# Linear attention and a two-layer feed-forward on one core: weight blocks kept for a third chunk, half of x without a trip through memory, one combination kept in PSUM, and a new hand-written order

## Chip, cores and metric

One Trainium2 chip, one core of it. The metric is the device time of one execution in microseconds (us). Kernel before: 828.3 us, the median of 3 runs (825.68 to 830.06). The profile and the trace are of one execution of 824.08 us, whose span is 822.3 us.

Names of the engines: PE is TensorE (matmuls), PEld its weight loads, DVE VectorE, ACT ScalarE, POOL GpSimd, SP the engine that issues every DMA of this kernel.

## What is computed

```python
def _attn_ref(q, k, v):                      # batch 8, heads 8, seq 576, head_dim 64
    q_s = np.exp(q - np.max(q, axis=-1, keepdims=True))
    q_s = q_s / (np.sum(q_s, axis=-1, keepdims=True) + 1e-09)
    k_s = np.exp(k - np.max(k, axis=2, keepdims=True))
    k_s = k_s / (np.sum(k_s, axis=2, keepdims=True) + 1e-09)
    kv = np.einsum('bhsd,bhse->bhde', k_s, v)
    return np.einsum('bhsd,bhde->bhse', q_s, kv)

def _moe_ref(x, w_in, w_out):                # x 4608 x 512, w_in 512 x 2048, w_out 2048 x 512
    h = x @ w_in
    g = np.where(h >= 1, h, np.where(h <= -1, 0.0, (h + 1) ** 2 / 4))
    return g @ w_out
```

The output of the attention, 4608 tokens by 512, is the x of the feed-forward. All of it is fp32.

## The kernel before

**The work.** The 4608 tokens go in 9 chunks of 512. An fp32 operand is split into a high and a low part (fp32r), and each product is made of three matmuls (high by high, high by low, low by high), so the feed-forward is 3168 matmuls of 128x512 on PE. w_in is cut into 16 blocks f of 512 KB (both parts), w_out likewise.

- *Chunk 0* makes the parts of the weights: `weights` (L561) loads raw w_in and w_out (`st<-in_w`), scales and splits them (ACT L614 the high part, POOL L618 the low part), and stores most blocks to memory. Blocks 1, 3, 5, 7, 9, 11 of w_in stay in rooms of SBUF that x will need later (HELD, L69) until chunk 1 has used them; the other ten are stored and loaded again for chunk 1, and all sixteen for chunk 2, `w<-b` (`fetch`, L671).
- *Chunks 0 to 2* are computed plainly: `first_layer` (matmuls L1499, bank h), the middle (relu ACT L1651, square ACT L1655 or POOL L1657, min and max DVE L1661), `second_layer` (split ACT L1684 and DVE L1687, matmuls L1696, banks o).
- *Chunks 3 to 8* go in pairs (3,4), (5,6), (7,8) by Strassen's scheme in Winograd's form, seven products in place of eight. `two_first_layers` (L1531) computes for each of 8 units p the products P1, P2, P5, P6, P3, P7, P4 into three PSUM banks: A is `h{p%2}`, C is `h{1-p%2}`, B is `hb`. In the notes of the trace they are hA, hC and hb. What is C for one unit is A for the next. DVE adds the results (L1582); `combinations` (L1737) does the same for the second layer (split L1786, L1789, matmuls L1801 into oA and oX, sums L1836).
- For this the sums of weight blocks are needed (`sums`, L757): sw, ss, then the split w_s (ACT L740, DVE or POOL L744), stored as s (L788) and loaded as `w<-s`. They are made in chunks 1 and 2 from the blocks that are in SBUF then.

**x.** `attention_two` (L1215) makes k's maxima (L1250), turns them (`mt`, L1256), stores them and loads them spread over the partitions (`mk<-mt` L1260, `m<-mk` L1268), subtracts (L1277), takes exp (L1283), sums kv on PE (L1293) and scales it (z L1304, L1306, kvt L881 and L879); `x_two` (L883) multiplies (L903). For chunks 3 to 8 x goes from PSUM to a tile xo (ACT L473 or DVE L475), from there to memory (`xk<-xo`, L936), and back into the five slots of xc, of which there is one buffer (`xc<-xk`, L1161); from xc come seven differences and copies (L1176), split into the rooms x0 to x13 (ACT L1188, DVE or POOL L1193).

**Buffers.** Five rooms of 512 KB serve w (pool ws); x rooms x0 to x13 hold x of chunks 0 to 2 (x0 to x3, x4 to x7, x10 to x13) and HELD blocks.

**The order.** The program first lists its operations with a home engine each, and then `Plan.settle` (L413) emits them in the order of a hand-written list, SEQUENCE, that holds the numbers of the operations of all engines in one row. A second list, SECOND, names those that go to their other engine. Nothing reorders at run time: an engine takes its operations in this order, and waits at each until what it needs is there.

```python
        for n in SECOND:
            self.ops[n].engine = self.ops[n].ways[1][0]
        done = set()
        for n in SEQUENCE:
            assert done.issuperset(d.n for d in self.ops[n].deps)
            done.add(n)
        return [self.ops[n] for n in SEQUENCE]
```

## Time and profile before

| | |
|---|---|
| median of 3 runs | 828.3 us (825.68 to 830.06) |
| profiled execution, its span | 824.08 us, 822.3 us |
| granted clock of PE, mean | 0.996 |
| PE busy | 792.0 us (96%) |
| PEld busy | 631.5 us (77%) |
| DVE busy | 605.8 us (74%) |
| ACT busy | 479.4 us (58%) |
| POOL busy | 439.7 us (53%) |
| DMA | 213.35 MB, 76.7% of 16 DMA engines' span in the main queue |

The table says which engines have much to do, not which one sets the end: a busy share is an average over chunk 0, the plain chunks and the pairs. Matmuls are pipelined and their ends are modelled, so "busy" of PE is not a measure of its pace. Which wait ends last is read from the timeline and the chain of waits.

### The profile page before, as it was taken

To read this page: it belongs to the slowest core of one execution; us is meant where nothing else is said; L and a number is where in the kernel's file an instruction comes from. 1 tells how busy PE (TensorE), PEld (TensorE's weight loads), DVE (VectorE), ACT (ScalarE), POOL (GpSimd) and SP (SyncE) were. 2 spreads that over 40 slices of the span, in tenths; PEclk is the share of its full clock that TensorE was granted. 3 is DMA by queue.
4 is the path that set the end of the run, shared out by engine and by line. 5 is a ranking of instruction groups with operands and counts; after the bars stand their busy time and mean duration, and the time that the engine had idled before them with its cause. 6 is when DMAs were issued, how large, how long until landed. Compare 5 with 4: busy or idle time off the path is not lost.

```text
span 822.3 us, 12384 instructions
## 1 busy us (share of the span) xinstructions
PE 792.0 (96%) x4136; PEld 631.5 (77%) x4136; DVE 605.8 (74%) x1024; ACT 479.4 (58%) x906; POOL 439.7 (53%) x358
## 2 busy tenths in 40 slices
PE   7999999999899999989999999999999999999997
PEld 6677777778586778767787778787877888888886
DVE  6787879777567767877877897778669764755684
ACT  6876865356545564567476755555657454455553
POOL 5545555354456656554666633474762644673633
PEclk9999999999999999999999999999999999999999
DMA  9788988888889897988898666686667675575546
GB/s 327 249 283 274 309 294 284 299 308 276 282 267 324 308 315 273 305 299 267 274 330 276 204 225 226 251 307 229 244 206 238 214 236 184 193 268 192 179 153 205
DMA packets 83232, 213.35 MB, mean 259 GB/s; under 512 B 9440, under 2 KB 17376, under 8 KB 83168
## 3 DMA queue, kind: packets, MB, share of 16 engines
q1 hardware_dynamic: 83168, 212.55, 76.7%
q8 instruction: 33, 0.54, 0.3%
q14 instruction: 31, 0.25, 0.1%
HBM read 165.31 MB, written 47.20 MB: 258 GB/s over the span
## 4 chain that ended last, share of the span: by engine, by line
PE 67%; DMA 16%; DVE 5%; ACT 4%; issue 3%; POOL 2%; SPq 2%; DVEq 0%; POOLq 0%; ACTq 0%
PE hA L1558 14%; PE oA L1801 14%; PE oX L1801 11%; PE h L1499 8%; PE hC L1558 8%; PE o L1696 6%; PE hb L1558 3%; DMA w<-s 3%; DMA st<-in_w 3%; PE x L903 2%; DMA q<-in_q 2%; DMA w_P<-v_P 1%; PE kv L1293 1%; DMA w<-b 1%; DMA m<-mk 1%
## 5 line engine op out<-in xcount | busy, mean ns | idle before, releaser
L1558 PE MATMUL hA<-x,w 128*128 128x512 f32 x576 | 144.6, 391 | 0.4 <-DMA w<-s 0.3
L1801 PE MATMUL oA<-g_P,w_P 128*128 128x512 f32 x576 | 141.1, 390 | 0.0
L1801 PEld LDWEIGHTS oA<-g_P,w_P 128*128 128x128 f32 x576 | 107.6, 188 | 24.1 <-ACT x L1188 0.8
L1558 PEld LDWEIGHTS hA<-x,w 128*128 128x128 f32 x576 | 107.6, 188 | 24.1 <-DMA w<-s 1.3
L1696 PE MATMUL o<-wh,g 128*128 128x512 f32 x384 | 119.9, 392 | 0.3 <-DVE g L1687 0.3
L1499 PE MATMUL h<-x,w 128*128 128x512 f32 x432 | 113.1, 395 | 2.0 <-ACT xo L473 1.2
L1789 POOL TENSOR_TENSOR g_P<-g,g_P 128x512 fp32r<-128x512 f32 x54 | 76.3, 1420 | 66.7 <-ACT g_P L1786 60.7
L1786 ACT CAST g_P<-g 128x512 fp32r<-128x512 f32 x120 | 72.9, 618 | 66.9 <-PE oA L1801 20.4
L1801 PE MATMUL oX<-g_P,w_P 128*128 128x512 f32 x432 | 106.7, 391 | 1.8 <-DMA w_P<-v_P 1.8
L1499 PEld LDWEIGHTS h<-x,w 128*128 128x128 f32 x432 | 80.4, 189 | 22.3 <-ACT xo L473 1.8
L1801 PEld LDWEIGHTS oX<-g_P,w_P 128*128 128x128 f32 x432 | 80.6, 188 | 20.1 <-ACT g_P L1786 2.5
L1696 PEld LDWEIGHTS o<-wh,g 128*128 128x128 f32 x384 | 72.5, 189 | 16.7 <-DVE g L1687 2.0
L1558 PE MATMUL hC<-x,w 128*128 128x512 f32 x288 | 74.3, 393 | 5.1 <-DMA w<-s 2.5
L1696 PE MATMUL o<-wl,g 128*128 128x512 f32 x192 | 76.4, 398 | 2.2 <-ACT g L1684 2.1
L1655 ACT ACTIVATE r<-r 128x512 f32<-128x512 f32 x109 | 68.4, 630 | 1.1
L1558 PEld LDWEIGHTS hC<-x,w 128*128 128x128 f32 x288 | 53.4, 188 | 19.5 <-DVE g L1661 3.0
L1657 POOL TENSOR_TENSOR r<-r 128x512 f32<-128x512 f32 x35 | 39.3, 1122 | 48.9 <-ACT r L1651 48.9
L1789 DVE TENSOR_TENSOR g_P<-g,g_P 128x512 fp32r<-128x512 f32 x66 | 52.8, 806 | 13.4 <-ACT g_P L1786 13.1
L1409 POOL TENSOR_TENSOR q<-q,qmb 128x512 f32<-128x512 f32 x32 | 37.4, 1181 | 40.3 <-DVE qmb L1391 35.6
L1409 POOL TENSOR_TENSOR q<-q,qzb 128x512 f32<-128x512 f32 x32 | 35.2, 1109 | 39.5 <-DVE qzb L1431 34.3
L1651 ACT ACTIVATE r<-c,half 128x512 f32<-128x512 f32 x48 | 34.2, 721 | 37.3 <-DVE c L1582 36.1
L1789 POOL TENSOR_TENSOR g_P<-c,g_P 128x512 fp32r<-128x512 f32 x27 | 38.0, 1410 | 28.3 <-ACT g_P L1786 28.2
(144 smaller groups left out, 1461.1 us busy)
## 6 DMA issues: line engine op xcount, KB each, us to landing
w_P<-v_P SPq DMA_DIRECT2D x84, 512.0 KB
w<-b SPq DMA_DIRECT2D x50, 512.0 KB
w<-s SPq DMA_DIRECT2D x48, 512.0 KB
st<-in_w SPq DMA_DIRECT2D x32, 512.0 KB
v<-in_v SPq DMA_DIRECT2D x32, 325.0 KB
q<-in_q SPq DMA_DIRECT2D x36, 256.0 KB
kt<-in_kt SPq DMA_DIRECT2D x32, 288.0 KB
...
```

The source lines that it names most:

```text
L903: nc.tensor.matmul(t[r][cols, :, p0:p1], kvt[rows, g % NKV, pr, :], q[pr]["tq"][rows, :, p0:p1], start=True, stop=True, tile_position=(r * ...
L1293: nc.tensor.matmul(kv[d, i, :], t[pr]["k"][:, j, d], t[pr]["v"][:, j, e * (D + 1) : (e + 1) * (D + 1)], start=(j == 0), stop=(j == KJ - 1) ...
L1409: nc.gpsimd.tensor_tensor(qf, qf, at, alu)
L1499: nc.tensor.matmul(t["h"], lhs, rhs, start=(turn == 0 and i == 0), stop=(turn == NPAIR - 1 and i == 2),)
L1558: nc.tensor.matmul(banks[b]["h"], lhs, rhs, start=(begins and not kk and not m), stop=(ends and kk == 1 and m == 2), skip_group_check=True,)
L1651: nc.scalar.activation(t["r"], t["h"], AF.Relu, bias=half[:, :1], scale=0.5)
L1655: nc.scalar.activation(t["r"], t["r"], AF.Square)
L1657: nc.gpsimd.tensor_tensor(t["r"], t["r"], t["r"], ALU.mult)
L1696: nc.tensor.matmul(outs[c, j], t["g"][:, k, s], rhs, start=(begins and i == 0), stop=(closes and i == 2),)
L1786: nc.scalar.copy(t["g"][:, 0, :], tile_of(i, b))
L1789: by(engine).tensor_tensor(t["g"][:, 1, :], tile_of(i, b), f32(t["g"][:, 0, :]), ALU.subtract)
L1801: nc.tensor.matmul(banks[side, d], wr[c, group, k, i // 2][:, i % 2, w, d * P : (d + 1) * P], t["g"][:, g, :], start=(begins and w == 1), ...
```

## The change

1. **KEPT.** Blocks 2, 4, 6, 8 of w_in are loaded in chunk 1 into x rooms 0 to 3 (which x of chunk 0 has left) and, with the held blocks 9 and 11, stay for chunk 2 (STAY). Six loads of 512 KB in chunk 2 are left out, and these blocks take none of the five rooms of w.
2. **Half of x straight.** For the first half (h = 0) of each chunk 3 to 8, ACT or DVE copies x from PSUM into its slot of xc (`x_straight`); 12 stores and 12 loads of 256 KB are left out. The one buffer of xc is taken from then on.
3. **12 stays in PSUM.** The sum P3 + U2 was written to a slot in SBUF, after which bank C was free. Now it is written in place in bank C, the middle for it reads PSUM and writes a slot, and bank C is free only after the min.
4. **More ways.** The low part of the weights (L618) and the row operations of q (L1409) may run on DVE: by the new SECOND 7 of 32 and 15 of 64 do. DVE has 1055 instructions where it had 1024, ACT 898 (901), POOL 328 (356), SP 574 (604). The matmuls are the same.
5. **A new order.** SEQUENCE and SECOND are new from end to end.

```diff
 HELD = {1: 10, 3: 11, 5: 12, 7: 13, 9: 8, 11: 9}
+KEPT = {2: 0, 4: 1, 6: 2, 8: 3}
+STAY = {9: 8, 11: 9, **KEPT}
...
 SEQUENCE = (
-    1, 0, 20, 86, 93, 44, 63, 11, 2, 19, 12, 43, 100, 3, 13, 62, 30, 4, 14, 31, 6, 21, 87, 88,
...
+    20, 1, 44, 0, 19, 86, 345, 93, 43, 63, 62, 11, 21, 30, 12, 100, 31, 54, 2, 3, 55, 32, 13,
...
-        def low():
+        def low(engine):
             hi, lo = parts()
-            nc.gpsimd.tensor_tensor(lo, whole(), f32(hi), ALU.subtract)
+            by(engine).tensor_tensor(lo, whole(), f32(hi), ALU.subtract)
...
-        g = op("POOL", 1.31, due, low, [e], port=True)
+        g = op("POOL", 1.31, due, low, [e], port=True, other=vector)
...
+    def fetch_kept(f, due):
+        r = ring(f"x{KEPT[f]}", 1)
...
+            wr[1, f] = wr[2, f] = flat.rearrange("p (q i t) -> p q i t", q=2, i=2)
+            nc.sync.dma_start(f32(wr[1, f]), blocks[f])
...
+        o = plan.read(0.45, due, emit, [made["stored", f], *r.wait()], 512)
...
             if c == 1 and f in HELD:
                 made[c, f] = made[f, 0]
+            elif c == 1 and f in KEPT:
+                made[c, f] = fetch_kept(f, due - 1.5 * STEP)
+            elif c == 2 and f in STAY:
+                made[c, f] = made[1, f]
             else:
...
+        def x_straight(r):
+            kk = two[r]
...
+            def emit(engine):
+                if c == base and not kk:
+                    xcs[base] = rp.tile([P, 5, T], F32, tag="xc", name=f"xc_{c}_0", bufs=1)
+                copy_by(engine, xcs[base][:, (3 * kk, kk + 1)[c - base], :], flat(r))
...
+            if not h:
+                rxc, begins = ring("xc", 1), c == base and not kk
+                waits = rxc.wait() if begins else [xdone[base, 0]]
+                ways = [("DVE", 0.69, False)]
+                xo = do("ACT", 0.59, due + 1, x_straight(r), xm, *waits, other=ways)
...
-        qs = do("POOL", 1.04, 1, q_rows("qm", ALU.subtract), qm, port=True)
+        qs = do("POOL", 1.04, 1, q_rows("qm", ALU.subtract), qm, port=True, other=vector)
...
-        c12, c22 = {}, {}
+        c22 = {}
...
-        o12 = dve(spilled(c12, "c12", s12), h["C"], lambda: side["U2"], due + 8.4, p3, u2, *r12.wait())
-        r12.take(o12)
-        rc.free(o12)
+        o12 = dve(h["C"], h["C"], lambda: side["U2"], due + 8.4, p3, u2)
...
-            for i, (x, b) in enumerate(((three, "12"), (four, "22"))):
-                d = middle(c + 1, f + i, due + 14 + 4 * i, *x[:2], kept=True)
-                unit[b] = x[0], d, x[2]
+            place = take_slot()
+            d = middle(c + 1, f, due + 14, *three, place=place)
+            ring(f"ps h{1 - p % 2}", 1).free(d)
+            unit["12"] = three[0], d, place
```

**What stands where, before and now.** Three places. The first is DVE's list of operations in chunk 1, about the step that scales kv of head group 4_0 (z, rz, kvt), for which PE waits with the next x. Before:

```order
L925 TENSOR_TENSOR x12_2472<-x_2_1_0_2453,x12_2472 128x512
L1424 TENSOR_REDUCE qs_4_0_2491<-q_4_0_2353 128x16
L1277 TENSOR_TENSOR k_3_3_2423<-k_3_3_2423,m2_3_1_2464 128x640
L1424 TENSOR_REDUCE qs_4_0_2491<-q_4_1_2368 128x16
L1304 TENSOR_SCALAR z_4_0_2536<-kv_4_0_2494 128x2
L1306 RECIPROCAL rz_4_0_2538<-z_4_0_2536 128x2
L881 TENSOR_SCALAR kvt_95<-kv_4_0_2494,rz_4_0_2538 128x64
L1661 SCALAR_TENSOR_TENSOR h_1_14_2409<-h_1_14_2409,r_1_14_2516 128x512
```

Now (in the changed file the lines are some 30 to 55 further down: L1353 is L1304, L1326 is L1277):

```order
L788 TENSOR_TENSOR sw_1_2490<-x0_1483 128x512
L1713 SCALAR_TENSOR_TENSOR h_1_14_2367<-h_1_14_2367,r_1_14_2426 128x512
L1353 TENSOR_SCALAR z_4_0_2521<-kv_4_0_2493 128x2
L1355 RECIPROCAL rz_4_0_2523<-z_4_0_2521 128x2
L905 TENSOR_SCALAR kvt_95<-kv_4_0_2493,rz_4_0_2523 128x64 x2
L1473 TENSOR_REDUCE qs_4_0_2531<-q_4_0_2378 128x16
L1739 TENSOR_TENSOR g2_1_14_2516<-h_1_14_2367,g2_1_14_2516 128x512
L1473 TENSOR_REDUCE qs_4_0_2531<-q_4_1_2411 128x16
L480 COPY qzo_4_0_2562<-qs_4_0_2531 32x32 x4
```

The subtraction of group 3_3 (`k_3_3<-k_3_3,m2_3_1`), which needs a load of m, stood ahead of z; now the two subtractions with m2_3_1 stand 15 and more rows behind it, and both halves of kvt are DVE's (one was ACT's).

The second place is SP's list at the start of the first pair. s7_0 and s7_1 are the stores of the last two weight sums; w_3_0_0 to w_3_0_3 are the weights of the pair's first unit (b0, s0_0, s0_1, b1), and xc_3_1 the second filling of xc. Before:

```order
L1240 DMA q_6_1_3654<-in_q 128x512
L1260 DMA mk6_0_176<-mt_6_0_3539 4x32
L788 DMA s7_1_144<-w_s_7_1_3634 128x1024
L675 DMA w_3_0_1_3668<-s0_0_129 128x1024
L1240 DMA v_6_0_3673<-in_v 128x650
L1268 DMA m2_6_0_3698<-mk6_0_176 128x256
L653 DMA v1_P2_153<-wh13_992 128x256
L675 DMA w_3_0_2_3712<-s0_1_130 128x1024
L675 DMA w_3_0_3_3714<-b1_114 128x512
```

Now:

```order
L811 DMA s7_0_143<-w_s_7_0_3490 128x1024
L811 DMA s7_1_144<-w_s_7_1_3511 128x1024
L685 DMA w_3_0_1_3542<-s0_0_129 128x1024
L1210 DMA xc_3_1_3555<-xk3_2_167 128x512
L663 DMA v1_P2_153<-wh11_963 128x256
L685 DMA w_3_0_0_3565<-b0_113 128x1024
L1210 DMA xc_3_1_3555<-xk3_3_168 128x512
L1309 DMA mk6_0_172<-mt_6_0_3581 4x32
L1210 DMA xc_3_1_3555<-xk4_2_169 128x512
L1309 DMA mk6_0_172<-mt_6_0_3581 4x32
L1210 DMA xc_3_1_3555<-xk4_3_170 128x512
L685 DMA w_3_0_2_3648<-s0_1_130 128x1024
```

Both stores and w_3_0_1 came to the front. Before, w_3_0_2 took the room that w_s_7_1 left and had to wait for the store s7_1 to land; now it is w_3_0_0, the block that the pair's very first matmuls read, and three of the loads of xc_3_1 stand behind it.

The third place is PE's list about the end of P3 (hC with x4, x5) of the pair's first unit and the next unit's P1 (hA with x0, x1), which writes into the bank that was C. Before:

```order
L1558 MATMUL hC_3_0_3729<-x4_3167,w_3_0_2_3712 128x512 x3
L1558 MATMUL hC_3_0_3729<-x5_3689,w_3_0_2_3712 128x512 x3
L1558 MATMUL hA_3_0_3705<-x10_3559,w_3_0_2_3712 128x512 x3
L1558 MATMUL hA_3_0_3705<-x11_3744,w_3_0_2_3712 128x512 x3
L1558 MATMUL hA_3_1_3792<-x0_2940,w_3_1_0_3736 128x512 x3
L1558 MATMUL hA_3_1_3792<-x1_3621,w_3_1_0_3736 128x512 x3
L1558 MATMUL hA_3_0_3705<-x12_3564,w_3_0_3_3714 128x512 x3
```

Now:

```order
L1612 MATMUL hC_3_0_3712<-x4_2961,w_3_0_2_3648 128x512 x3
L1612 MATMUL hC_3_0_3712<-x5_3681,w_3_0_2_3648 128x512 x3
L1612 MATMUL hb_3_1_3758<-x2_3276,w_3_1_0_3679 128x512 x3
L1612 MATMUL hb_3_1_3758<-x3_3627,w_3_1_0_3679 128x512 x3
L1748 MATMUL o_2_2_2851<-wl14_970,g2_2_14_3591 128x512
L1748 MATMUL o_2_2_2851<-wh14_969,g2_2_14_3591 128x512 x2
L1612 MATMUL hA_3_0_3620<-x12_3540,w_3_0_3_3667 128x512 x3
L1612 MATMUL hA_3_0_3620<-x13_3738,w_3_0_3_3667 128x512 x3
L1748 MATMUL o_2_1_2759<-wl15_972,g2_2_15_3629 128x512
L1748 MATMUL o_2_1_2759<-wh15_971,g2_2_15_3629 128x512 x2
L1612 MATMUL hA_3_1_3807<-x0_2755,w_3_1_0_3679 128x512 x3
```

Between the end of P3 and the next unit's P1 stood 6 matmuls; now 18 stand there. Over the 21 such hand-overs of the three pairs it was 0 once, 6 three times, 12 five times, and 18 or 24 the other twelve times; now it is 12 once (between units 3 and 4 of the pair (5,6)), 18 four times, and 24 to 54 the other sixteen times. For the other bank, from the end of P4 to the next unit's P5, it was 12 at the least (twice); now it is 6 once (between units 1 and 2 of the pair (3,4), with one group of kv matmuls beside them), and 12 twice. In the one list of all engines' operations, 24 matmuls stand between the store s7_1 and the first P1 of the pair (3,4).

## Rows read from the trace of the kernel before

**Rows 1.** The page: busy time by engine; DMA share in 40 slices, tenths
```profile
PE 792.0 (96%) x4136; PEld 631.5 (77%) x4136; DVE 605.8 (74%) x1024; ACT 479.4 (58%) x906; POOL 439.7 (53%) x358
...
DMA  9788988888889897988898666686667675575546
```
**Rows 2.** One window of 50 us: us, busy (x instructions) by engine, clock, DMA share, GB/s
```profile
650.00:700.00 50.00, 50.00 (x221) 41.21 (x220) 28.06 (x44) 24.68 (x43) 23.01 (x18) 1.00 0.63 205
```
**Rows 3.** Timeline near 220 us: start, us, engine, line, operation, count [idle before <-releaser]
```profile
220.08 0.82 DVE L1277 TENSOR_TENSOR k<-k,m 128x640 f32<-128x640 f32 x1 [3.27 <-DMA m<-mk]
...
221.42 0.15 DVE L1304 TENSOR_SCALAR z<-kv 128x2 f32<-128x2 f32 x1
...
222.55 0.54 PE L903 MATMUL x<-ta,kvt 64*64 64x192 f32 x2 [2.47 <-ACT kvt L879]
```
**Rows 4.** Chain of waits, DMA pieces of it in order of time: start us, us
```profile
143.81 4.74 DMA s<-w_s
148.61 5.53 DMA w<-b
...
257.90 4.69 DMA xk<-xo
...
328.56 4.23 DMA s<-w_s
332.86 6.00 DMA w<-s
```
**Rows 5.** Timeline near 155 us and near 263 us
```profile
154.87 0.68 DVE L765 TENSOR_TENSOR sw<-x 128x512 f32<-128x512 f32 x1
...
156.21 0.50 PE L1499 MATMUL h<-x,x 128*128 128x512 f32 x1 [1.99 <-DVE g L1687]
...
262.66 0.59 ACT L473 COPY xo<-x 128x512 f32<-128x512 f32 x1 [1.47 <-DMA xk<-xo]
...
263.30 1.43 PE L1499 MATMUL h<-x,w 128*128 128x512 f32 x5 [1.23 <-ACT xo L473]
```
**Rows 6.** Timeline, PE's waits for weights in the pairs
```profile
335.19 0.50 PE L1558 MATMUL hC<-x,w 128*128 128x512 f32 x1 [0.48 <-DMA w<-s]
...
338.99 0.47 PE L1558 MATMUL hC<-x,w 128*128 128x512 f32 x1 [0.77 <-DMA w<-s]
...
487.52 0.47 PE L1558 MATMUL hC<-x,w 128*128 128x512 f32 x1 [1.30 <-DMA w<-s]
...
633.61 0.47 PE L1801 MATMUL oX<-g_P,w_P 128*128 128x512 f32 x1 [1.58 <-DMA w_P<-v_P]
```
**Rows 7.** Timeline near 360 us: one bank's middle behind k's subtraction
```profile
357.29 1.10 DVE L1277 TENSOR_TENSOR k<-k,m 128x640 f32<-128x640 f32 x1 [1.75 <-DMA k<-in_k]
...
362.07 0.50 PE L1558 MATMUL hC<-x,w 128*128 128x512 f32 x1 [2.14 <-DVE g L1661]
```
**Rows 8.** Groups of instructions: shapes xcount | busy us, mean ns | idle before, releaser
```profile
L1661 DVE SCALAR_TENSOR_TENSOR c<-c,r 128x512 f32<-128x512 f32 x48 | 43.7, 912 | 4.3 <-POOL r L1657 2.5 <-ACT r L1655 1.8
...
L1661 DVE SCALAR_TENSOR_TENSOR g<-hA,r 128x512 f32<-128x512 f32 x24 | 16.5, 687 | 16.8 <-ACT r L1655 9.8 <-POOL r L1657 6.9
L1582 DVE TENSOR_TENSOR c<-hC,sn_P 128x512 f32<-128x512 f32 x24 | 16.4, 684 | 10.4 <-PE hC L1558 9.1 <-ACT sn_P L473 1.3
...
L1651 ACT ACTIVATE r<-c,half 128x512 f32<-128x512 f32 x48 | 34.2, 721 | 37.3 <-DVE c L1582 36.1
L1657 POOL TENSOR_TENSOR r<-r 128x512 f32<-128x512 f32 x35 | 39.3, 1122 | 48.9 <-ACT r L1651 48.9
...
L1558 PE MATMUL hC<-x,w 128*128 128x512 f32 x288 | 74.3, 393 | 5.1 <-DMA w<-s 2.5 <-DVE g L1661 2.1 <-ACT sn_P L473 0.4
```
**Rows 9.** Timeline: PE's first wide matmul, and two waits in chunk 0
```profile
24.73 0.96 PE L1499 MATMUL h<-x,w 128*128 128x512 f32 x3
...
64.22 0.73 PE L1499 MATMUL h<-x,x 128*128 128x512 f32 x2 [1.42 <-DVE z L1304]
...
96.89 0.47 PE L1696 MATMUL o<-wl,g 128*128 128x512 f32 x1 [1.31 <-ACT g L1684]
```

More of the change, by code (lines that the diff above doesn't have):

```diff
@@ L475, in copy_by, with by @@
             nc.vector.tensor_copy(out, src)
+    vector = [("DVE", 0.69, True)]
+    def by(engine):
+        return nc.vector if engine == "DVE" else nc.gpsimd
     half = const.tile([P, 32], F32, name="half")
@@ L700, in pool_or_vector @@
         return op("POOL", 1.85 * us, due, emit, deps, port=True, other=[("DVE", us, True)])
-    def by(engine):
-        return nc.vector if engine == "DVE" else nc.gpsimd
     def staged(t, key, p, name):
@@ L1123, in attention @@
         rqz.take(qr)
[L1124 removed]
+        qn = do("POOL", 1.04, 3, q_rows("qrz", ALU.mult), qz, port=True, other=vector)
         rqz.free(qn)
```

59 lines of the change are left out of this document (40 added, 19 removed), and 489 rows, old and new, of tables (SECOND, SEQUENCE).

## The prediction, made before the changed kernel was run

> **What bounds the kernel now.** I read the page first, then windows of the span, then PE's timeline for gaps, and the chain of waits for what released them. PE is busy for 96% of the span, DVE for 74%, and the DMA share is 0.8 to 0.9 in the first half and falls after that [rows 1]. Busy PE is not PE at pace, so I look for a stretch that is: from 650 to 700 us PE takes 221 matmuls in 50 us, all of them wide ones, so one costs 0.226 us [rows 2]. The 3168 wide ones need 717 us at that pace. The change takes none of them away, so it can only act on the other 105 us of the span: the start (the first wide matmul begins at 24.73 [rows 9]), the small matmuls of x and kv, the tail, and PE's waits. What a reader should see in rows 3 to 9 is that no single engine makes these waits. Each is a late transfer, or an engine that takes its list in order and stands at an operation that is not ready while the one PE needs is behind it. A new order can take such waits away, and make others like them.
>
> **Part by part.** A minus is time won.
>
> *k's subtraction ahead of z.* DVE stands 3.27 us at k_3_3's subtraction for the load of m, with z, rz and kvt behind it, and PE waits 2.47 us for kvt [rows 3]. In the new order both subtractions with this m stand 15 rows and more behind z. Term: -2.5; ends -2.5 and -1.0, the latter if another late operation stands there.
>
> *Half of x straight.* The copy of x_4_0 into xo waits for the store of the x before it (4.69 us [rows 4]), and PE waits 1.23 us for the bank [rows 5]. That copy is of a first half, which now goes to xc and waits for no store: -1.2. The copies themselves stay as many; 12 stores and 12 loads fall away, which PE only feels as earlier landings of others. A new wait could come from xc, taken earlier: I see no reader of the old filling that is late, 0.
>
> *Six weight loads less, four rooms.* In chunk 1 a block's load had to wait until a store had emptied its room: 4.74 us for the store, 5.53 for the load, the two in a row in the chain [rows 4]. DVE then stood at that block's sum, the split of g came late, and PE waited 1.99 us [rows 5]. Blocks 2, 4, 6 and 8 now have rooms of their own, and the others come round later. Term -2.0, ends -2.0 and 0.
>
> *Start of the first pair.* PE waited 0.48 and 0.77 us for w_3_0_1 and w_3_0_2 [rows 6]; both loads are now placed further ahead: -1.2. But now w_3_0_0 is the load that has to wait for the store s7_1. Store and load took 4.23 and 6.00 us, 10.2 together [rows 4], and in the list 24 matmuls, 5.4 us, stand between that store and the first matmul that reads the block. If the store is issued where the list has it, PE waits 4.8 us there; if POOL is early with the last sum by as much, nothing. I take +3.0, nearer the wait, as POOL's sum itself stands only a few matmuls ahead of the store; ends 0 and +4.8. Behind that load on SP stand three loads of xc_3_1 and the stores of k's maxima. They are late by the same time, and what needs them comes after the same wait, so I add nothing. The Trainium skill ("SBUF — State Buffer", section on the DMA setup-cost knee) gives a transfer some 2 us plus its bytes at 436 GB/s; by that, as an estimate, store and load of 512 KB would take 6.4 us and PE would wait 1.0. The rows here say 10.2, with the queues as full as they are in this half, and I go by them.
>
> *Later waits for weights.* 1.30 us at 487.52 and 1.58 us at 633.61 [rows 6]. The traffic there is a little less and the order is new; neither is a reason for all of it. Term -1.4, half; ends -2.9 and 0.
>
> *A bank behind k's load.* DVE stood 1.75 us for k, and the next unit's C came 2.14 us late [rows 7]. The k loads of that group are not clearly earlier now. Term -1.0, ends -2.1 and +1.
>
> *Chunk 0 and the start.* PE's two longest waits in chunk 0 are 1.42 and 1.31 us, for z and for a split g behind the making of the weights [rows 9]. Seven of POOL's low parts go to DVE and the shortest distance from a bank's last matmul to its next first one grows. Term -1.4; ends -2.7 and +1. The start is rearranged, q's loads ahead of v's: -1.0, ends -3 and +3 (an eighth of 24.73 either way).
>
> *12 in PSUM.* The sum is written to PSUM (684 ns as before) and not to a slot. Its min then reads a bank and one tile in SBUF and should cost what the other banks' cost, 687 ns where the min with both inputs in SBUF has 912 [rows 8]: 24 times 0.225 us, 5.4 us less on DVE. Against it stand 22 operations that DVE takes over from POOL; the nearest price is that 912: 20 us more. So DVE gets some 15 us busier in 822, 2%, spread over a queue with a quarter of its time free: 0 by itself. What counts is bank C. It was free after the sum; now relu (0.72), square (1.12 on POOL) and min (0.69) come on top [rows 8]: 0.68 + 0.72 + 1.12 + 0.69 is 3.2 us after the end of P3. The new order leaves 12 matmuls (2.7 us) once, 18 (4.1 us) four times, 24 and more (over 5.4 us) sixteen times. The first is short by 0.5 us; at the four, 0.9 us is left for two engines' queues. Term +1.5; ends 0 and +9 (below).
>
> *Other waits of a new order.* All terms above are of waits that I can name; a list that is new from end to end will have some of its own. I count them by having taken half where I saw no reason for all.
>
> **Sum.** -2.5 -1.2 -2.0 -1.2 +3.0 -1.4 -1.0 -1.4 -1.0 +1.5 = -7.2 us. From the profiled execution's 824.1 us that is 816.9. The median of the runs is 828.3, 4.2 above the profiled one, so I put the median after at **821** us.
>
> **Rivals.**
>
> *No change (827).* The waits move instead of going: only those with a reason in the order (-2.5, -1.2) are won, and w_3_0_0 (+3.0) eats most of it. For it: the DMA share in the second half is 0.6 to 0.7 [rows 1, 2], where six loads less can't be what PE waits for. Against it: the waits of rows 3 and 5 are 5.7 us and their causes are removed one by one.
>
> *Slower through bank C (834).* The next unit's P1 waits for DVE's min. It decides when a min comes more than 0.9 us late, after DVE stood at something else, as in rows 7, where bank A's middle took PE 2.14 us in just this way. With DVE 2% fuller and P1 a taker of the bank, as P5 is for the other, five hand-overs (12 and 18 matmuls) at 2.1 us cost 10.5, in place of my +1.5: 824.1 - 7.2 + 9 = 825.9 profiled, 830 as a median; with w_3_0_0 at its full 4.8 and a wait of this size at three more hand-overs, 838. I put 834, between the two. Against it: hC had the same dependence on a min in all 21 hand-overs of the other bank and lost only 2.1 us of its 5.1 to DVE's g [rows 8]. The Trainium skill ("Perfetto Trace Analysis", "Matmuls") wants independent groups to rotate through PSUM banks, so that the emptying of one lies beside the next group's matmuls. Holding C through its middle goes against that rule.
>
> *More is won (812).* All named waits go (-2.5 -1.2 -2.0 -1.2 -2.9 -2.1 -2.7 -1.0 = -15.6) and neither w_3_0_0 nor bank C costs anything.
>
> **How the numbers follow.** Two runs of this kernel differ by some 0.5%, 4 us, which is what a measurement can tell. Chances: forecast 0.48 (815 to 826), more won 0.17, no change 0.19, slower by bank C or by a like wait of the new order 0.16. The range from **811 to 833** leaves out half of the slower case and a little below. Faster by over 0.5% means under 824.2: the case of more, and 0.43 of the forecast, 0.60. Within 0.5%: 0.24. Over 832.4: 0.16.
>
> **What would show it.** Right: near 220 us x follows kv with no wait for kvt over 0.5 us; no copy of a first half of x waits for a store; PE's first P1 at the pair's start waits 1 to 5 us for w_3_0_0; its waits on hA for DVE's min add up to 2 us or less over the three pairs; the min of 12 lasts 0.69 us. Wrong: P1 waiting for a min in most units, a DVE queue that is late at z or at the split of g all through chunks 1 and 2, or a start that ends after 26 us.

## The result, and the profile after

The changed kernel takes **808.8 us** (median of 4 runs, 807.95 to 810.57), the kernel before 829.2 beside it (825.68 to 831.09): ratio 0.976 [0.972, 0.980], 20 us less. In a later series on another chip the ratio was 0.980 [0.976, 0.983] (`a_again` below), so the gain is 16 to 20 us. Times are medians without slow runs, of which five of the variants below had one each. I had said 821 and 811 to 833: the direction was right, the size less than half, and the time lies below the range.

The profiled execution of the changed kernel took 808.96 us, that of the kernel before 824.08, 15.1 us more. First the page; the rows of before are [rows 1].

```profile
PE 787.0 (97%) x4136; PEld 630.5 (78%) x4136; DVE 609.8 (76%) x1055; ACT 478.8 (59%) x903; POOL 397.6 (49%) x330
...
DMA  9877988998788878988686687756667467655546
...
q1 hardware_dynamic: 78848, 203.11, 74.0%
...
PE 79%; DMA 8%; DVE 5%; ACT 3%; issue 2%; POOL 1%; SPq 0%; DVEq 0%; POOLq 0%; ACTq 0%
```

Read it as before: busy shares tell little. DVE has 4 us more and POOL 42 less, and that decides nothing (`a_pool`). The last line says more: it is the share of the chain that ended last, by engine. DMA holds 8% of it, where it held 16% before. The main queue moved 203.1 MB; it was 212.6.

Where the time came from is seen by cutting the span. PE's busy time (first number with an "x" behind it) in four stretches; first the kernel before, then the changed one:

```profile
125.00:230.00 105.00, 99.52 (x607) 78.43 (x607) 78.76 (x151) 54.05 (x108) 51.85 (x48) 0.98 0.84 283
230.00:315.00 85.00, 83.40 (x484) 65.76 (x479) 60.87 (x108) 46.10 (x95) 51.71 (x46) 1.00 0.90 309
315.00:480.00 165.00, 160.52 (x873) 127.24 (x873) 133.31 (x214) 104.34 (x200) 94.63 (x72) 1.00 0.83 277
480.00:640.00 160.00, 157.12 (x750) 125.99 (x749) 123.50 (x207) 95.02 (x180) 82.17 (x64) 1.00 0.71 241
```

```profile
125.00:230.00 105.00, 104.97 (x655) 83.67 (x654) 83.08 (x153) 58.19 (x112) 58.29 (x55) 1.00 0.90 307
230.00:315.00 85.00, 84.52 (x482) 67.43 (x478) 70.01 (x136) 47.93 (x97) 40.56 (x37) 1.00 0.83 282
315.00:480.00 165.00, 164.81 (x895) 131.72 (x895) 136.50 (x232) 106.84 (x203) 76.67 (x59) 1.00 0.79 271
480.00:640.00 160.00, 158.51 (x754) 126.52 (x753) 119.91 (x187) 94.48 (x182) 88.61 (x69) 1.00 0.63 213
```

From 125 to 230 us (chunk 1 and the start of chunk 2) PE was idle for 5.5 us and is now for 0.03; from 315 to 480 it was 4.5 and is 0.2. The stretches hold slightly different work, as the changed kernel runs ahead, so only PE's idle time in them is compared. I added up over PE's timeline how much later each wide matmul starts than the one before it plus 0.226 us [rows 2], small matmuls apart. These waits fell from 28.2 to 17.9 us (-10.3); the 17 groups of x matmuls with what stands ahead of them from 24.9 to 20.0 (-4.9, of it -3.3 in the one group of [rows 3]); the first wide matmul came at 23.72 in place of 24.73 (-1.0); the kv groups and the tail each took 0.5 more. Together -15.2, with the rounding of each; it was 15.1. (Pauses of PE over 0.15 us alone, from the first wide matmul on, add up to 19.8 us before and 9.0 now; below they are called PE's pauses.)

Not all of this is waiting. In the first row of before the granted clock is 0.98. The lost part lies right behind the wait of 1.99 us [rows 5], where PE runs at 0.50, the lower of its two levels (1.2 and 2.4 GHz). The same 3.4 us, before and now:

```profile
156.70:160.10 3.40, 3.40 (x10) 2.62 (x9) 2.57 (x4) 0.62 (x1) 2.31 (x3) 0.50 0.91 348
```

```profile
156.70:160.10 3.40, 3.40 (x16) 2.82 (x15) 3.33 (x7) 1.78 (x3) 1.30 (x2) 1.00 0.99 356
```

Ten matmuls stand where 16 do now: about half of the 3.4 us, 1.7 us, goes to the clock beside the 1.99 of the wait. Not every wait of PE has this behind it (the 2.47 us of [rows 3] and the 2.14 of [rows 7] do not), and the changed kernel has one such stretch too, from 64.8 us in chunk 0, so the two profiles, apart from their start, lose the same by it. The runs do not: in the series of `a_again` the granted clock has a median of 0.989 for the kernel before (11 runs) and 0.9975 for the changed one (6). If PE had work all the while that the clock was low, 0.0085 of some 820 us, up to 7 us of the 16 between the medians there, would be clock. This is an estimate; no run holds the clock fixed, so the share is not shown.

The place of [rows 3], PE's and DVE's timeline where kv of head group 4_0 is scaled:

```profile
212.62 1.39 PE L1342 MATMUL kv<-v,k 128*64 128x65 f32 x40
...
214.31 0.14 DVE L1353 TENSOR_SCALAR z<-kv 128x2 f32<-128x2 f32 x1
214.48 0.17 DVE L1355 RECIPROCAL rz<-z 128x2 f32<-128x2 f32 x1
214.68 0.48 DVE L905 TENSOR_SCALAR kvt<-kv,rz 128x64 f32<-128x64 f32 x2
...
216.20 0.38 PE L927 MATMUL x<-ta,kvt 64*64 64x192 f32 x2
```

No row has a bracket, so nobody waits: z comes 0.3 us after kv, and x follows when PE has done its other work. The copy of a first half of x no longer waits 1.47 us for a store [rows 5], and the start of the pair (3,4) has no wait for a block:

```profile
250.85 0.59 ACT L478 COPY xc<-x 128x512 f32<-128x512 f32 x1 [0.42 <-PE x L927]
...
303.30 2.45 SPq L811 DMA_DIRECT2D s<-w_s  x2
...
310.07 0.32 SPq L685 DMA_DIRECT2D w<-b  x1
...
314.99 0.47 PE L1612 MATMUL hA<-x,w 128*128 128x512 f32 x1
```

The groups, against [rows 8]:

```profile
L1612 PE MATMUL hA<-x,w 128*128 128x512 f32 x576 | 146.3, 392 | 0.0
...
L1612 PE MATMUL hC<-x,w 128*128 128x512 f32 x288 | 73.5, 391 | 0.7 <-DVE sn_P L480 0.6
...
L1713 DVE SCALAR_TENSOR_TENSOR g<-hC,r 128x512 f32<-128x512 f32 x24 | 16.4, 685 | 7.7 <-POOL r L1709 4.8 <-ACT r L1707 2.7
...
L1326 DVE TENSOR_TENSOR k<-k,m 128x640 f32<-128x640 f32 x28 | 24.2, 869 | 0.2
```

The min of 12 reads a bank and lasts 685 ns (912 before [rows 8]; 687 was forecast). P1, which now waits for it, loses 0.0 us over all three pairs: bank C is free in time at each of the 21 hand-overs. Matmuls on hC lose 0.7 where it was 5.1. And DVE stands 0.2 us ahead of k's subtractions; in the kernel before it stood there for 8.9.

### The profile page after: what moved, and what is told of

It reads as the page before. It is cut to its first block, busy times and chain, and to the rows that moved or that the text cites. A ratio compares the mean times of both kernels' runs of the same rounds, so it can differ in the third digit from the quotient of the medians.

```text
span 807.2 us, 12301 instructions
## 1 busy us (share of the span) xinstructions
PE 787.0 (97%) x4136; PEld 630.5 (78%) x4136; DVE 609.8 (76%) x1055; ACT 478.8 (59%) x903; POOL 397.6 (49%) x330
## 4 chain that ended last, share of the span: by engine, by line
PE 79%; DMA 8%; DVE 5%; ACT 3%; issue 2%; POOL 1%; SPq 0%; DVEq 0%; POOLq 0%; ACTq 0%
PE hA L1612 16%; PE oA L1853 16%; PE oX L1853 11%; PE o L1748 11%; PE h L1548 10%; PE hC L1612 8%; PE hb L1612 4%; DMA st<-in_w 3%; PE kv L1342 2%; PE x L927 2%; DMA q<-in_q 2%; DVE st L601 1%; DMA w_P<-v_P 1%; DMA xc<-xk 1%; DMA v_P<-w_v 1%
## 5 line engine op out<-in xcount | busy, mean ns | idle before, releaser
L1841 POOL TENSOR_TENSOR g_P<-g,g_P 128x512 fp32r<-128x512 f32 x66 | 91.1, 1385 | 128.9 <-ACT g_P L1838 122.4
L1838 ACT CAST g_P<-g 128x512 fp32r<-128x512 f32 x144 | 88.2, 619 | 65.5 <-PE oA L1853 25.6
L1548 PE MATMUL h<-x,w 128*128 128x512 f32 x312 | 79.7, 392 | 1.5 <-DVE g L1739 1.0
L1709 POOL TENSOR_TENSOR r<-r 128x512 f32<-128x512 f32 x42 | 46.1, 1100 | 67.2 <-ACT r L1703 62.3
L1841 DVE TENSOR_TENSOR g_P<-g,g_P 128x512 fp32r<-128x512 f32 x78 | 62.1, 800 | 15.8 <-ACT g_P L1838 15.2
L1548 PE MATMUL h<-x,x 128*128 128x512 f32 x264 | 71.2, 397 | 0.0
L1548 PEld LDWEIGHTS h<-x,w 128*128 128x128 f32 x312 | 58.1, 188 | 16.1 <-DVE g L1739 2.2
L1548 PEld LDWEIGHTS h<-x,x 128*128 128x128 f32 x264 | 49.9, 191 | 11.4 <-issue 0.5
L1748 PEld LDWEIGHTS o<-wl,g 128*128 128x128 f32 x192 | 36.2, 188 | 14.5 <-issue 4.4
L1458 POOL TENSOR_TENSOR q<-q,qmb 128x512 f32<-128x512 f32 x24 | 29.5, 1233 | 35.6 <-DVE qmb L1440 33.7
```

The lines of the kernel that those rows point to most:

```text
L1458: by(engine).tensor_tensor(qf, qf, at, alu)
L1548: nc.tensor.matmul(t["h"], lhs, rhs, start=(turn == 0 and i == 0), stop=(turn == NPAIR - 1 and i == 2),)
L1709: nc.gpsimd.tensor_tensor(t["r"], t["r"], t["r"], ALU.mult)
L1748: nc.tensor.matmul(outs[c, j], t["g"][:, k, s], rhs, start=(begins and i == 0), stop=(closes and i == 2),)
L1838: nc.scalar.copy(t["g"][:, 0, :], tile_of(i, b))
L1841: by(engine).tensor_tensor(t["g"][:, 1, :], tile_of(i, b), f32(t["g"][:, 0, :]), ALU.subtract)
```

## Experiments

Sixteen more kernels ran. Every ratio is against the kernel before, measured beside it on the same chip. Where a variant has operations that its list of numbers lacks, or lacks some that the list has, the list was mended by a rule and not tuned: a new load stands some 45 places ahead of its first reader, and what would stand ahead of an operation it depends on is put just behind that.

### The kernel before once more

`b_again` has no edit.

> The kernel before, unchanged. The profiled execution of before took 824.1 us and lies below all four timed runs (825.7 to 831.1), while the changed kernel's profiled execution (809.0) lies inside its runs (808.0 to 810.6). Theory 1: the kernel before varies by its waits for transfers, and that profile shows a lucky execution; then this one's profile is of 825 to 831 us, and what it has more than the first, 1 to 7 us, is idle time of PE released by loads or by operations behind a load. Theory 2: the profiled execution is shorter by something else than waits; then the idle times of PE by releaser agree with those of the first profile within 1 us.

825.6 us (818.96 to 829.29, 10 runs), ratio 0.999 [0.996, 1.002]. Waits come back at their places: 1.99 us at 155.96, 2.28 at 362.26, 0.88 at 485.72, 1.39 at 631.51, and the x group of [rows 3] is 4.55 us again (4.44). Together 26.3 us ahead of wide matmuls (28.2). So most of them are made by the order and are no accident of one execution; the one of [rows 5] near 263 us is 0.49 us here (1.39). This profile was again of a short execution (822.6 where the median is 825.6), so what a long one has more was not seen. That matters for my sum, below.

### Parts without the order, order without the parts

`e_order`: the changed kernel with its parts undone (six blocks loaded again, both halves of x through memory, 12 written to a slot), in the new order and with its choice of engines. `e_parts`: the kernel before with all parts, in its own order and with its own choice of engines.

```diff
 e_order, against the changed kernel
-KEPT = {2: 0, 4: 1, 6: 2, 8: 3}
-STAY = {9: 8, 11: 9, **KEPT}
+KEPT = {}
+STAY = {}
-            if not h:
+            if False:
-        o12 = dve(h["C"], h["C"], lambda: side["U2"], due + 8.4, p3, u2)
+        o12 = dve(spilled(c12, "c12", s12), h["C"], lambda: side["U2"], due + 8.4, p3, u2, *r12.wait())
```

> The order alone: blocks 2, 4, 6, 8, 9, 11 are loaded again in chunk 2, all of x goes through memory, 12 is spilled to a slot, as before; the order and the engines are those of the changed kernel, with the 30 operations that it lacks put in (a load about 45 places of the list ahead of its first use), and a few operations set back where a buffer asks for it. Theory A, the order carries the gain (operations that are late no longer stand ahead of those that PE needs): 809 to 816 us. Theory B, the parts carry it (the waits come from the loads and stores that the parts leave out): 822 to 832 us. Between these, both are needed.

> The parts alone: blocks kept, half of x straight, 12 in PSUM, in the order and on the engines of the kernel before, with operations set back only where a buffer asks for it (the next unit's P1 behind the min of 12 in 5 or so units). Theory A, the order carries the gain: 822 to 832 us, since the subtraction ahead of z and the waits in chunk 1 stay, and only the wait for the store of x goes (1.4 us). Theory B, the parts carry it: 809 to 817 us.

`e_order` 905.6 us, ratio 1.094 [1.089, 1.098]; `e_parts` 850.2, 1.029 [1.025, 1.032]. Both are far slower than the kernel before and beyond any range that was expected: there is no "gain of the order" and "gain of the parts" that add up. The groups of PE say why. In `e_order`:

```profile
L1547 PE MATMUL h<-x,w 128*128 128x512 f32 x432 | 120.7, 413 | 27.4 <-ACT xo L480 15.7 <-DVE g L1740 11.7
...
L1749 PE MATMUL o<-wl,g 128*128 128x512 f32 x192 | 80.0, 417 | 13.1 <-ACT g L1737 11.1 <-DVE wl L630 1.1 <-POOL q L1457 0.9
```

The new order has the copies of a first half of x where nothing holds them up; with the trip through memory put back, a copy waits for a store, and PE for the copy. Its matmuls are slower as well (413 and 417 ns; 392 and 398 in the changed kernel), at a mean granted clock of 0.962: as an estimate, 0.038 of 904.5 us, up to 34 us, is lost to the clock, beside PE's pauses of 78.9 us. How much of both comes from the places that the rule gave to what was put back is not known. In `e_parts` PE waits instead on hA:

```profile
L1609 PE MATMUL hA<-x,w 128*128 128x512 f32 x576 | 149.8, 398 | 20.4 <-DVE g L1710 7.6 <-DMA w<-b 7.5 <-DVE c L1633 3.1
```

7.6 us are for a min (nine times) and 7.5 for `w<-b` (three times, 4.57 of it at the pair's start). Each list is written for its own set of dependences.

### Each part alone in the old order

`p_straight`, `p_kept` and `p_psum` have one part each.

```diff
 p_straight (with x_straight and the waits for xc, as in the change)
+            if not h:
+                xo = do("ACT", 0.59, due + 1, x_straight(r), xm, *waits, other=ways)
 p_kept (with fetch_kept)
+KEPT = {2: 0, 4: 1, 6: 2, 8: 3}
+STAY = {9: 8, 11: 9, **KEPT}
 p_psum (with the middle of 12 from its bank)
-        o12 = dve(spilled(c12, "c12", s12), h["C"], lambda: side["U2"], due + 8.4, p3, u2, *r12.wait())
+        o12 = dve(h["C"], h["C"], lambda: side["U2"], due + 8.4, p3, u2)
```

> One part alone, in the order of the kernel before: the first halves of x of chunks 3 to 8 go straight to xc, 12 stores and 12 loads of 256 KB fall away. Theory A, what this part gives by itself is the wait for the store of x near 263 us and a little of the waits for weights: 1 to 3 us faster, 822 to 825 us against some 826. Rival, the transfers left out carry much of the whole gain by themselves: 5 us or more, under 821 us. Rival 2, nothing: the wait moves to the next thing that is late.

> One part alone, in the order of the kernel before: blocks 2, 4, 6, 8 in rooms x0 to x3 in chunks 1 and 2, 9 and 11 stay; six loads of 512 KB less. The five rooms of w then go round in another sequence, and two loads (that of block 2 in chunk 1, and w_3_0_0) are set back where a buffer asks for it. Theory A, by itself this part takes away the wait in chunk 1 near 156 us (2 us) and brings the wait for w_3_0_0 at the start of the first pair (4.7 us in the kernel with all three parts): 826 to 831 us. Rival, the traffic that is left out is what counts: under 822 us.

> One part alone, in the order of the kernel before: 12 stays in PSUM, so the next unit's P1, for which 0 to 24 matmuls were left after P3 in that order, waits for the min (operations set back only where the buffer asks for it). Theory A, bank C is a real price that the new order pays by putting 12 and more matmuls in between: with relu, square and min behind the sum, some 3 us, ten or so of the 21 hand-overs are short by 0.5 to 3 us; 12 to 20 us slower, 838 to 846 us, with PE's waits at hA released by DVE's sum and min. Rival, the mins come in time and what made the parts alone 24 us slower is another part: under 830 us.

| | us | ratio |
|---|---|---|
| `p_straight` | 827.5 | 1.000 [0.997, 1.003] |
| `p_kept` | 833.0 | 1.010 [1.006, 1.014] |
| `p_psum` | 843.9 | 1.019 [1.016, 1.023] |

`p_straight`: 6.3 MB less in the queue, no first half of x that waits for a store, and no gain. Its profile says why in part: PE's pauses are 20.3 us (19.8 before), with 2.08 at 159.58 for z, 3.00 at 225.79 for kvt and 2.30 at 367.19 for a min, the waits of [rows 5, 3, 7] at their places. So these waits, which the order makes, are paid without those transfers too. `p_kept` loses the wait of [rows 5] near 155 us and is slower all the same, in the main by the wait that I had feared at the pair's start. SP's issues (the store s7_1, then the load of w_3_0_0) and PE:

```profile
328.12 0.39 SPq L810 DMA_DIRECT2D s<-w_s  x1
...
332.35 0.32 SPq L684 DMA_DIRECT2D w<-b  x1
...
336.11 0.70 PE L1608 MATMUL hA<-x,w 128*128 128x512 f32 x1 [4.44 <-DMA w<-b]
```

The load is issued when the store has landed, 4.23 us after it, and PE goes on 3.76 after that: 8.0 for both, where I had taken 10.2 from other places. The wait of 4.44 is near the upper end I had given it. The Trainium skill ("SBUF — State Buffer", DMA setup-cost knee) gives for both, as an estimate from its figures, 6.4; the rows here decide.

`p_psum` is the bank C rival itself. PE's group, and one hand-over:

```profile
L1608 PE MATMUL hA<-x,w 128*128 128x512 f32 x576 | 148.7, 395 | 14.7 <-DVE g L1709 7.8 <-DVE c L1632 2.9 <-DVE g L1804 1.4
```

```profile
542.64 0.68 DVE L1632 TENSOR_TENSOR hC<-hC,sn_P 128x512 f32<-128x512 f32 x1
...
543.36 0.69 ACT L1699 ACTIVATE r<-hC,half 128x512 f32<-128x512 f32 x1 [4.55 <-DVE hC L1632]
...
544.12 1.04 POOL L1705 TENSOR_TENSOR r<-r 128x512 f32<-128x512 f32 x1 [0.85 <-ACT r L1699]
...
545.19 0.69 DVE L1709 SCALAR_TENSOR_TENSOR g<-hC,r 128x512 f32<-128x512 f32 x1 [0.60 <-POOL r L1705]
...
545.94 0.50 PE L1608 MATMUL hA<-x,w 128*128 128x512 f32 x1 [1.25 <-DVE g L1709]
```

Sum, relu, square and min follow each other with hardly a gap, 542.64 to 545.88, 3.2 us as reckoned, and the P1 of the next unit waits at the end of the row. In the kernel before hA lost 0.4 us, here 14.7.

### A few operations moved in the old order

`b_ksub` moves one subtraction of k (and its exp) behind kvt, nothing else:

```diff
-    ... 1038, 1148, 1152, 1026, 1028, 1151, 1078, 1064, 1113, 1065, 1066, 1106, 1154, 1046, 1149, 1134,
+    ... 1038, 1148, 1026, 1028, 1151, 1078, 1064, 1113, 1065, 1066, 1106, 1046, 1149, 1152, 1154, 1134,
```

> The kernel before with one operation moved: the subtraction of group 3_3 (and the exp behind it) stands behind z, rz and kvt of group 4_0 and behind the next subtraction, where it stood ahead of z. Theory A, a late operation at the head of DVE's list is what PE waits for: the wait of 2.5 us for kvt near 220 us goes and the profiled execution is 2 to 3.3 us shorter than before's, 0.3 to 0.4% of the time. Rival: the wait is made up for or moves on to the next thing that is late (the exp, the kv of group 3_1): less than 0.5 us.

823.9 us, 0.997 [0.995, 1.000]: 2.2 us, with an interval of 0.4 to 3.9, where I had priced it at 2.5. In its timeline DVE still stands at the subtraction for the load of m, though for 0.35 us only, and PE has its kvt by then:

```profile
221.29 1.56 DVE L1277 TENSOR_TENSOR k<-k,m 128x640 f32<-128x640 f32 x2 [0.35 <-DMA m<-mk]
...
221.33 0.38 PE L903 MATMUL x<-ta,kvt 64*64 64x192 f32 x2
```

`b_moves` moves seven of the kernel's operations: those two, two steps of a weight sum near 155 us behind the z and the split of g that stood after them ([rows 5]), two operations on k at 357 us behind the bank's min ([rows 7]), and the load w_3_0_1 ahead of others (not in the diff here).

```diff
-    567, 827, 929, 706, 818, 782, 930, 697, 781, 819, 663, 850, ...
+    567, 827, 706, 818, 782, 697, 781, 819, 663, 929, 930, 850, ...
...
-    1759, 1753, 1803, 1565, ... 1764, 1800, 1773, 1805, 1774, 1755, 1767, ...
+    1759, 1753, 1565, ... 1764, 1773, 1774, 1755, 1803, 1805, 1800, 1767, ...
```

> The kernel before with seven operations moved in its list and nothing else: the subtraction ahead of z of group 4_0 (as in b_ksub), two subtractions of k behind the min of bank A that they stood ahead of (362 us), two sums of weight blocks behind a split of g and z that they stood ahead of (156 us), and the load w_3_0_1 further ahead. Theory A, the waits are made by the order and go when the late operation steps back: 2.2 + 2.1 + 2.0 + 0.5 us, 6 to 7 us faster, 0.8%. Rival, what is taken from one wait comes back at the next: less than 3 us.

820.4 us, 0.992 [0.988, 0.995], 7 us less, as expected, with not one byte or operation saved and without any of the parts. PE's waits of 2.47, 1.99 and 2.14 us [rows 3, 5, 7] are gone. At the last of the three places DVE now reads:

```profile
356.60 0.68 DVE L1661 SCALAR_TENSOR_TENSOR g<-hA,r 128x512 f32<-128x512 f32 x1
357.19 1.83 DVE L1277 TENSOR_TENSOR k<-k,m 128x640 f32<-128x640 f32 x2
```

The bank's min comes first, and k when it is there. So single operations that stand unready at the head of an engine's list cost about what the trace says. Something came in their place all the same:

```profile
170.19 0.96 PE L1499 MATMUL h<-x,w 128*128 128x512 f32 x3 [1.35 <-DVE g L1687]
...
337.64 1.62 PE L1558 MATMUL hC<-x,w 128*128 128x512 f32 x6 [2.13 <-DMA w<-s]
```

The first is new, the second stands where PE waited 0.48 and 0.77 us [rows 6]. PE's pauses fell by 4.9 us (19.8 to 14.9), not by the 6.6 of the three waits, and the profiled execution is 5.0 us shorter (819.04). The low clock behind the wait of [rows 5] went with it.

### One part out of the changed kernel

`a_nopsum` writes 12 to a slot again, `a_nostraight` sends the first halves through memory, `a_nokept` has no KEPT and STAY (edits as in `e_order`, one each).

> The changed kernel with one part undone: 12 is spilled to a slot again, bank C is free after the sum; the order is the same list. Theory A, in the new order the part neither costs nor gives a wait, its gain is DVE's time (24 mins at 0.69 in place of 0.91 us): DVE is 4 to 6 us busier, and the time is 809 to 812 us. Rival, bank C's holding still costs PE 1 us or more in the changed kernel: 806 to 808 us without it.

> The changed kernel with one part undone: the first halves of x go through the one tile xo to memory and back; 12 stores and 12 loads are put back into the new list (a store right behind its copy). Theory A, the new order counts on a copy that waits for no store: the second copy of each pair waits 4 to 5 us for the store of the first, with the bank and PE behind it; with the order alone that was 25 us over seven waits, so 825 to 838 us. Rival, the order has room for it: under 815 us.

> The changed kernel with one part undone: all blocks but the six held ones go through the five rooms of w, and six loads of chunk 2 are put back into the new list, about 45 places ahead of their first use or where their room allows it. Theory A, the new order counts on the four rooms: loads come late, the sums of weights that stand ahead in DVE's list hold back the splits of g, and PE waits 40 to 60 us in chunks 1 and 2: 850 to 880 us. Rival, only the order of x needs its part: under 820 us.

| | us | ratio |
|---|---|---|
| `a_nopsum` | 810.3 | 0.979 [0.975, 0.983] |
| `a_nostraight` | 838.4 | 1.011 [1.007, 1.016] |
| `a_nokept` | 876.5 | 1.058 [1.054, 1.063] |

Without 12 in PSUM nothing changes, though DVE has 10 us more to do (619.7). The other two are needed by this list. Where `a_nostraight` loses:

```profile
259.57 0.58 ACT L480 COPY xo<-x 128x512 f32<-128x512 f32 x1 [6.50 <-DMA xk<-xo]
...
260.21 0.63 PE L1547 MATMUL h<-x,x 128*128 128x512 f32 x1 [5.12 <-ACT xo L480]
```

ACT stands 6.5 us at one copy for a store, and PE 5.1 behind it; at 372.68 the same again, 5.40 for a copy on DVE. In `a_nokept` it is the split of g behind late blocks, worst at

```profile
180.04 0.79 PE L1748 MATMUL o<-wl,g 128*128 128x512 f32 x1 [8.82 <-ACT g L1736]
```

Both times are in the main the price of a dependence for which a list has no room; both lists were mended by rule, and the bytes that came back were not priced apart here. The mean granted clock is lower as well, 0.985 and 0.968 (0.997 in the changed kernel).

### The bytes by themselves

The list of the changed kernel leaves room, so bytes can be added without a dependence. `a_traffic` adds 18 copies of 512 KB from one place in memory to another that nobody reads or waits for, at the places where the loads and stores were left out; the queue's bytes are then those of before, 212.55 MB. `a_tiny` has the same 18 issues with 4 KB each.

```diff
+    def copy_more(f, name, due, after):
+        def emit():
+            to = dp.tile([P, 2, 2, HT], F32, name=f"more_{name}")
+            nc.sync.dma_start(to, blocks[0])
+        plan.save(0.45, due, emit, [after], 512)
...
+                copy_more(f, f"w{f}", due, made["stored", 0])
...
+                copy_more(0, f"x{c}_{kk}", due, xo)
```

> The changed kernel with the bytes that it leaves out put back as bytes alone: 18 copies of 512 KB from memory to memory (9.4 MB) on the same queue, near the places of the six loads and of the 24 transfers of x; nothing reads them and nothing waits for them. Theory A, the parts help by waits that they take away and not by bytes: under 2.5 us slower than the changed kernel, up to 811 us. Rival, the time of the transfers is what counts: 5 us or more, over 813.5 us, with PE waiting for loads in chunks 1 and 2.

> As a_traffic, the same 18 copies at the same places, but of 4 KB in place of 512 KB. Theory B, the bytes count: within 2 us of the changed kernel (807 to 811 us). Rival, what counts is 18 more issues on SP's queue and their turn in it: 5 us or more slower, over 813.5 us, as with the full copies.

`a_traffic` 817.7 us (814.01 to 822.15), 0.987 [0.983, 0.992]; `a_tiny` 807.0, 0.978 [0.973, 0.982], like the changed kernel. The issues cost nothing that shows, the bytes about 8 us; by the two ratios, which are of different chips, it can be 2 to 13. The rows show where: a transfer that others wait for lands later.

```profile
275.41 0.58 ACT L479 COPY xo<-x 128x512 f32<-128x512 f32 x1 [4.30 <-DMA xk<-xo]
276.05 1.16 PE L1558 MATMUL h<-x,x 128*128 128x512 f32 x3 [2.33 <-ACT xo L479]
```

```profile
230.00:315.00 85.00, 80.77 (x442) 63.13 (x441) 66.78 (x130) 44.70 (x92) 38.36 (x35) 0.98 0.88 304
```

Between 230 and 315 us the DMA share is 0.88 (0.83 in the changed kernel) and PE is busy for 80.8 us (84.5), at a granted clock of 0.98: about half of the loss of the profiled execution (815.8 against 808.96) lies there. Later PE waits 1.83 us at 376.45 behind DVE, which stood 2.26 us at k's maxima for a load of kt. The wait for `w<-b` at the pair's start, 1.32 us here, is not the bytes' doing: `a_again` has 1.46 without them. A copy reads and writes memory, where a load that was left out only read it (53.5 MB are written here, 47.2 in the kernel before), so the 8 us may be more than those bytes are worth.

### What did not matter

`a_pool` sends the 22 operations of point 4 back to POOL; `a_moves` moves in chunk 0 a split of g and two mins (with the high part behind each) ahead of the shift of raw weights they stood behind; `a_again` is the changed kernel once more.

```diff
 a_moves
-    ... 503, 541, 525, 419, 527, 542, 533, 528, 478, 454, 532, 554, 453, 479, 529, ...
+    ... 503, 541, 525, 419, 527, 478, 542, 479, 533, 528, 454, 532, 554, 453, 529, ...
```

> The changed kernel with the 22 operations that it gave to DVE back on POOL (7 low parts of weights, 15 row operations of q), the same order. Theory, POOL's waits for them were hidden but its place in the list counts: a low part takes 1.3 us in place of 0.7 and is waited for in chunk 0; 1 to 5 us slower, 810 to 814 us. Rival, DVE, 76% busy, is relieved by it: up to 2 us faster, 806 to 808 us.

> The changed kernel with three places of chunk 0 mended by what the runs so far showed: a split of g (block 8) and two mins (blocks 11, 13) step ahead of the shift of raw weights that waits for its load, with the high part behind each min. Theory A, waits of PE of 0.96, 0.93 and 0.83 us go: 1.5 to 2.7 us faster than the changed kernel, 806 to 808 us. Rival, in chunk 0 the loads of raw weights are the pace, and what is won is waited for at the next block: within 1 us of it.

> The changed kernel itself, on the same chip as the three others: 807 to 811 us, 0.976 of the kernel before. Its second profile shows which of its waits come again in the same place (those in chunk 0 do, by the order; those for w_P may not).

809.4 us (0.979 [0.975, 0.983]), 811.7 (0.982 [0.977, 0.986]) and 811.1 (0.980 [0.976, 0.983]): three times the changed kernel, as far as the intervals tell. The choice of engines gives nothing that shows. In `a_moves` the three waits are gone and others have come (1.15 us at 97.95, 1.08 at 106.93); in the changed kernel's timeline DVE stands at the shift of a raw block that has not landed, and g and PE are behind it:

```profile
80.91 0.43 DVE L598 TENSOR_SCALAR st<-st 128x512 uint32<-128x512 uint32 x1 [1.96 <-DMA st<-in_w]
81.25 0.68 DVE L1739 TENSOR_TENSOR g<-h,g 128x512 fp32r<-128x512 f32 x1
...
81.99 0.50 PE L1548 MATMUL h<-x,w 128*128 128x512 f32 x1 [0.96 <-DVE g L1739]
```

That the arrival of the raw blocks sets the pace of chunk 0 fits this and the missing gain; no run changed those loads, so it is not shown. In `a_again` one wait is there that the first profile did not have, at the start of the pair:

```profile
316.50 0.70 PE L1612 MATMUL hA<-x,w 128*128 128x512 f32 x2 [1.46 <-DMA w<-b]
```

No variant beat the changed kernel clear of noise; the intervals of all that were level with it overlap its own.

## Why the prediction was wrong in size

**What was right.** k's subtraction ahead of z: -2.5 forecast, -3.3 in the group of x, 2.2 us (0.4 to 3.9) when moved alone. The copy of a first half of x and the wait in chunk 1: both gone. The min from PSUM: 687 ns forecast, 685 measured. Bank C's chain of 3.2 us, and that it decides when a list leaves P1 too close: `p_psum`. The start came out at the -1.0 forecast by luck: `b_again`, with no edit, begins its wide matmuls at 23.60 us, as early as the changed kernel (step 5).

**Steps that failed.**

1. *"I count them by having taken half where I saw no reason for all."* Half fits hardly any of the named waits. The bank behind k's load went whole (2.14 us to none; I had -1.0), and the x groups apart from the one of [rows 3] gave 1.6 for which I had no term. PE's waits for weights' loads went from 4.7 to 2.2, near the -2.6 of my two terms, but come back in part (`w<-s` 1.44 us at 473.25 and `w_P` 0.86 at 616.15 in `a_again`). Chunk 0 won nothing (7.7 to 8.6; I had -1.4). So a wait that one late operation makes goes whole when that operation is moved, as the three in `b_moves` did, though some of it can come back elsewhere. That a wait for a transfer goes by what its queue is relieved of fits the rest, and was not tried. I should have priced the two kinds apart.

2. *"I take +3.0, nearer the wait, as POOL's sum itself stands only a few matmuls ahead of the store"*, for w_3_0_0. I read places in one list of all engines as times. 24 matmuls stand between store and P1 in the list; in the run the store went out at 305.43 and P1 began at 314.99, 9.6 us or 42 matmuls. POOL and SP were 4 us ahead of their place: nothing in the list kept them from coming early. So the term was 0 in the profile. The wait is real, though: 1.46 us in another execution of the same kernel (`a_again`), and 4.44 in `p_kept`, where PE was ready for P1 3.6 us after the store went out.

3. *"Term +1.5"*, for bank C. It cost 0.0 in the profile of the changed kernel, and one wait of 0.66 us for a min at 372.41 in that of `a_moves`. `p_psum` has 14.7 us of waits on hA, most of them for the same dependence. In the order before, 9 of the 21 hand-overs have 12 matmuls or fewer between P3 and P1; in the new one 20 have 18 or more, and taking 12 out of PSUM again (`a_nopsum`) gains nothing. The Trainium skill ("Perfetto Trace Analysis", "Matmuls") wants independent groups to rotate through banks, so that the emptying of one lies beside the next one's matmuls. `p_psum` agrees with it; in the new order other matmuls cover the emptying, and holding the bank longer costs nothing that shows.

4. *"12 stores and 12 loads fall away, which PE only feels as earlier landings of others"*, and six weight loads with them, priced at the waits they stood in. In the new order 9.4 MB of unread copies cost about 8 us (2 to 13). I had argued against bytes by the DMA share of 0.6 to 0.7 in the second half; half of the loss lies between 230 and 315 us, where it is 0.88. How far these 8 us lie in the terms of the sum or beside them was not separated; the rows of `a_traffic` show waits for late transfers that come back with the bytes.

5. *"The median of the runs is 828.3, 4.2 above the profiled one, so I put the median after at 821 us."* I carried this over to the changed kernel, whose profile is 808.96 against a median of 808.78: nothing. In `b_again` the offset is 3. This step alone is 4 of the 12 us by which the 821 missed. What goes with it is on record: the granted clock, 0.996 and 0.997 in the two profiled executions of the kernel before, with a median of 0.990 over the 68 runs of it that list one; on the whole, the longer runs have the lower clock. One place of it is the start, where `b_again`, before and `b_ksub` have the same list:

```profile
12.70:22.90 10.20, 7.36 (x91) 4.97 (x91) 9.88 (x31) 10.14 (x25) 6.69 (x7) 1.00 0.91 345
```

```profile
12.70:22.90 10.20, 7.63 (x75) 5.46 (x77) 8.70 (x28) 9.05 (x21) 6.44 (x7) 0.83 0.89 345
```

```profile
12.70:22.90 10.20, 8.45 (x63) 6.24 (x67) 9.01 (x26) 8.24 (x19) 7.12 (x7) 0.50 0.86 310
```

The first wide matmul begins at 23.60, 24.73 and 26.97 us. In the changed kernel and `a_again` the clock in this window is 1.00 and that matmul begins at 23.72 and 23.95. So the profile that the sum began from was of an execution with little lost to the clock, and a term for the clock was missing; that the new start keeps the clock up in every run is likely from these, not shown.

The 12 us between 821 and 808.8 are thus about 4 of the offset, 3 of w_3_0_0, 1.5 of bank C, 1.3 of the bank behind k's load, 1.6 of the x groups, 0.8 of k's subtraction and 1.7 of the low clock that went with the wait at 156 us, less 2.3 of chunk 0 (-1.4 forecast, +0.9 measured, with the low clock from 64.8 us in it); what is left is under 1 us. The rival "more is won" had the right picture, and at 812 the nearest time; it too took chunk 0 for won and the offset for a constant.

**What stays open.** How much of the gain is clock and how much is waits, and what lowers the clock after some waits and not after others. Why the 6.3 MB less of `p_straight` show nowhere, when 9.4 MB more in the new order cost 8 us. And what share of the gain each part has in the new order, as `e_order`, `a_nostraight` and `a_nokept` were mended by rule.

## What to carry to other kernels

Where engines take their work in a fixed order, look for the one operation that stands unready at the head of a list while what another engine needs is behind it: its wait can be had by moving it alone (7 us here for seven moves, though some of the wait came back elsewhere). Look at the granted clock behind the wait, too: PE can pay more than the wait's length. A change that adds a dependence has to be tried with an order that leaves room for it; all parts cost 2.9% in the old order and are part of a 2% gain in the new one, so trying a part without the order can say the opposite of what it is worth. And price bytes in the stretch where DMA is fullest, not by its mean; `a_traffic` is one run that points to this.
